# Five buffers for the broadcast reciprocals, earlier key loads and shifted key pooling in a fused attention and MoE kernel

## The chip, the cores and the metric

The kernel runs on one core of one Trainium2 chip. Times are device microseconds of one execution. Before and after were timed several times on the same chip; all times below are of executions in the fast state unless a sentence says otherwise. Engines: PE is TensorE (matmul), DVE is VectorE, ACT is ScalarE, POOL is GpSimd, SP is SyncE. In this kernel POOL and SP matter for what they issue: POOL issues every load that casts from float32 to bf16, and SP issues the transposing reads of the queries. In the traces each works through its instructions in program order: below, three loads go out right behind a broadcast that waited 1.79 us.

## The reference, cut to what matters

```python
def _attn_ref(q, kv, w_sr):                # q: 4 x 12288 x 128, kv: 4 x 384 x 32 x 128
    kv_pool = kv.reshape(B, H // r, r, W // r, r, C).mean(axis=(2, 4))   # r = 4
    k = v = kv_pool.reshape(B, -1, C) @ w_sr                             # 768 keys per batch
    s = scale * (q @ k.transpose(0, 2, 1))
    a = np.exp(s - s.max(-1, keepdims=True)); a /= a.sum(-1, keepdims=True) + 1e-09
    return a @ v
def _moe_ref(x, w_in, w_out):              # x: 49152 x 128, w_in: 128 x 2048
    h = x @ w_in
    return (h * (1.0 / (1.0 + np.exp(-1.702 * h)))) @ w_out
```

## The kernel before

The 49152 queries are worked through in 96 groups of 512. A batch has 24 groups, a block has 4. All attention comes first, then all of the MoE stage. While the groups of batch b run, the keys of batch b+1 are prepared: six loads of a chunk each, two poolings of three chunks, and for each pooling a transpose and the products with `w_sr`. The parts that the change and the argument touch:

```python
kvload = ctx.enter_context(tc.tile_pool(name="kvload", bufs=3))     # raw keys: three chunks
qpool  = ctx.enter_context(tc.tile_pool(name="qpool", bufs=3))      # transposed queries, a block each
agpool = ctx.enter_context(tc.tile_pool(name="ag", bufs=15))        # exponentials
npool  = ctx.enter_context(tc.tile_pool(name="norm", bufs=3))       # reciprocals
# ...
def load_kv(b, a, ch):            # POOL queue, casts
    t = xs[NS - 1 - a * HC - ch] if b == 0 else kvload.tile([128, SG], BF, name="kvt")
    nc.gpsimd.dma_start(out=t, in_=kv_r[b, a, ch])
# ...
def cast_q(s):                    # POOL queue, casts a block of queries, HBM to HBM
    nc.gpsimd.dma_start(out=q_bf[sl, :]..., in_=q_flat[sl, :]...)
def load_qT(s):                   # SP queue, reads a cast block transposed
    qTs[s] = qpool.tile([128, 1, SG], BF, name="qT")
    nc.sync.dma_start_transpose(out=qTs[s], in_=q_bf[s * SG:(s + 1) * SG, :])
# ...
def sums(s):                      # after each block: sums of exponentials, reciprocals
    # ... 24 matmuls, DVE transpose, reciprocal, DVE transpose ...
    for gi in range(4):
        rb = npool.tile([128, 512], F32, name="rb")
        nc.gpsimd.partition_broadcast(rb, t2[32 * gi:32 * gi + 1, :])
        rb_of[4 * s + gi] = rb    # read later: x = av * rb, on DVE
loads = (5, 6, 7, 12, 13, 14)     # group of the batch at which each load is issued
def background(i):
    if i % 4 == 0:
        if 3 <= s + 2 < NS: load_qT(s + 2)
        if 4 <= s + 3 < NS: cast_q(s + 3)
    if b + 1 < B and gb in loads:
        a, ch = divmod(loads.index(gb), HC)
        load_kv(b + 1, a, ch)
# ...
for a, gbs in enumerate(((10, 12, 13, 14), (17, 18, 20, 21))):
    for gb, f in zip(gbs, (pool_kv, transpose_pooled, make_k, make_v)):
        steps[gb] = (f, a)
```

With three reciprocal buffers, the fourth broadcast of a block has to wait until DVE has used the first one. Whatever stands behind it on POOL waits as well.

The softmax here doesn't subtract the row's maximum and nothing guards it: scores larger than these inputs give would overflow.

## Time and profile before

| | before |
|---|---|
| time, first three executions | 1038.17, 1038.11, 1031.79 us |
| profiled execution | 1035.4 us, span 1033.6 us |
| attention, to the start of the last sums | 334.0 us |
| rest (almost all MoE) | 699.6 us |
| two blocks with the pooling of keys 0 to 383 | 22.2 and 17.1 us, against 13.0 in batch 1 |

The page of the kernel before, in four lines: span, busy times, granted PE clock in 40 slices, and the shares of the chain that ended last.

```profile
span 1033.6 us, 13286 instructions
PE 1000.9 (97%) x5298; PEld 458.1 (44%) x5398; DVE 262.3 (25%) x417; ACT 958.7 (93%) x709; POOL 98.2 (9%) x151
PEclk9999989999999999999999999999999999999999
...
PE 90%; DMA 5%; ACT 1%; DVE 1%; issue 1%; POOL 1%; ACTq 0%; POOLq 0%; DVEq 0%
```

PE bounds the kernel, and 5% of the chain is DMA. To find where, I cut attention into blocks, from the start of one block's sums (line 234) to that of the next. The table of stretches gives, for each stretch, its length, busy time and count of each engine, granted clock, DMA share and GB/s. The first two rows are attention and the rest, the other two the long blocks.

```profile
0.00:334.03 334.03, 310.04 (x1864) 132.35 (x1896) 123.66 (x216) 269.55 (x198) 95.27 (x147) 0.99 0.71 114
334.03:1033.61 699.58, 690.85 (x3436) 325.76 (x3504) 138.69 (x201) 689.14 (x512) 2.92 (x4) 1.00 0.10 37
121.48:143.67 22.19, 16.13 (x83) 6.18 (x84) 5.14 (x8) 11.34 (x9) 3.96 (x6) 0.85 1.24 128
206.42:223.56 17.14, 13.60 (x84) 5.61 (x86) 5.14 (x8) 11.20 (x9) 3.96 (x6) 1.00 1.22 145
```

A block without key work takes 11.93 us, one with a pooling 12.96. Only these two stand out; in the first the clock also falls to 0.85. The list of waits between 100 and 240 us says what PE waits for there (total us, times, longest), and the timeline of PE shows the first place.

```profile
PE ring L83 <- DMA kvt<-in_kv_dram: 9.2, 4, 4.9
```

```profile
130.76 0.39 PE L83 MATMUL ring<-kvt,mean 128*32 128x512 bf16 x1
132.00 0.38 PE L83 MATMUL ring<-kvt,mean 128*32 128x512 bf16 x1 [0.85 <-DMA kvt<-in_kv_dram]
137.31 1.86 PE L83 MATMUL ring<-kvt,mean 128*32 128x512 bf16 x10 [4.94 <-DMA kvt<-in_kv_dram]
139.11 1.46 PE L210 MATMUL big<-qT,kT 128*128 128x512 bf16 x3
```

The pooling has to wait for its second and third chunk. After the long wait three score matmuls take 1.46 us instead of the usual 0.81. The Trainium skill ("TensorE: Matmul & The Clock Gate", Part 1) says that an idle window of about 3.4 us halves the PE clock until it has been busy again for as long. Here the trace agrees: the granted clock is 0.50 from 136.11 us, 3.7 us into the idle time, to 142.94 us, and the 2.76 us wait in batch 3 has no such tail.

Why the chunks are late shows on the queues. First POOL between 113 and 120 us (start, duration, what, count, and in brackets the idle time before with what ended it), then the query transpose on SP at that time (start, and how long its issue record lasts), then the landing times of the three loads (least, median, greatest).

```profile
113.00 1.45 POOL L246 PARTITION_BROADCAST rb<-t  x2 [6.57 <-DVE t L243]
114.61 0.80 POOL L246 PARTITION_BROADCAST rb<-t  x1 [0.16 <-DVE x L226]
117.20 0.80 POOL L246 PARTITION_BROADCAST rb<-t  x1 [1.79 <-DVE x L226]
117.83 1.63 POOL L71 DMA_DIRECT2D kvt<-in_kv_dram  x3
119.41 0.55 POOL L117 DMA_DIRECT2D q_bf<-in_q_dram  x1
```

```profile
118.28 20.77 SPq L122 DMA_TRANSPOSE qT<-q_bf  x1
```

```profile
DMA to landing us min/median/max: 5.5/13.6/18.4
```

The fourth broadcast waits 1.79 us for DVE to free a buffer. The three loads follow it at once, 0.54 us apart. The query transpose starts 0.45 us after the first of them. The first load still lands after 5.5 us; the third takes 18.4 us, and the transpose's issue lasts 20.77 us, where 4 to 5 us is common. In batch 1 the same three loads go out 2.1, 1.5 and 1.0 us ahead of the transpose, and land after 5.5, 7.5 and 10.5 us.

### The profile page before, as it was taken

The page shows a single profiled execution, that of the slowest core. Times are in us where ns is not written, and L with a number is a line of the kernel's source. Part 1 is how long each engine was busy: PE and PEld are TensorE (multiplying, and loading weights), DVE is VectorE, ACT ScalarE, POOL GpSimd, SP SyncE. Part 2 cuts the span into 40 slices and gives each one's busy share as a digit, 9 for nine tenths or more (in the row PEclk, how much of TensorE's full clock was granted, in tenths as well). Part 3 has the DMA queues.
Part 4 walks back from the last instruction along what each step waited for, and adds up shares of the span by engine and source line. Part 5 has one row for each costly group of instructions (what it writes and reads, how often), then busy time and mean ns, then how long its engine had stood idle before and what let it go on. Part 6 is the DMA issues. An engine that isn't in the chain of part 4 may idle for free.

```text
span 1033.6 us, 13286 instructions
## 1 busy us (share of the span) xinstructions
PE 1000.9 (97%) x5298; PEld 458.1 (44%) x5398; DVE 262.3 (25%) x417; ACT 958.7 (93%) x709; POOL 98.2 (9%) x151
## 2 busy tenths in 40 slices
PE   6899979989999999999999999999999999999998
PEld 2344434434444444444444444444444444444443
DVE  3344324334333211211212112121121121211212
ACT  3888958978999999999999999999999999999997
POOL 2232322323222100000000000000000000000000
PEclk9999989999999999999999999999999999999999
DMA  9885798599520011011011010010110101101011
GB/s 197 153 146 99 107 103 157 78 148 143 94 50 1 11 42 41 32 40 42 33 39 42 31 41 37 36 41 31 42 41 32 42 31 41 41 31 42 31 42 41
DMA packets 67231, 63.85 MB, mean 62 GB/s; under 512 B 50176, under 2 KB 51328, under 8 KB 66816
## 3 DMA queue, kind: packets, MB, share of 16 engines
q0 software_dynamic: 7440, 26.22, 14.8%
q1 hardware_dynamic: 59728, 36.77, 14.5%
q8 instruction: 42, 0.69, 0.3%
q14 instruction: 21, 0.17, 0.1%
HBM read 52.49 MB, written 36.70 MB: 86 GB/s over the span
## 4 chain that ended last, share of the span: by engine, by line
PE 90%; DMA 5%; ACT 1%; DVE 1%; issue 1%; POOL 1%; ACTq 0%; POOLq 0%; DVEq 0%
PE big L287 32%; PE ring L301 31%; PE ring L222 11%; PE big L210 10%; DMA kvt<-in_kv_dram 3%; PE ring L234 3%; PE ring L313 2%; DMA x<-in_kv_dram 2%; ACT ag L290 1%; PE ring L83 1%; DVE x L226 1%; ACT ag L213 1%; POOL x L71 0%; POOL rb L246 0%; POOL kvt L71 0%
## 5 line engine op out<-in xcount | busy, mean ns | idle before, releaser
L290 ACT ACTIVATE ag<-big 128x1536 bf16<-128x1536 f32 x512 | 689.3, 1557 | 4.7 <-PE big L287 4.6
L287 PE MATMUL big<-x,w_in_sb 128*128 128x512 bf16 x1507 | 412.7, 379 | 2.2
L301 PE MATMUL ring<-ag,w_out_sb 128*128 128x512 bf16 x1496 | 407.1, 379 | 1.9 <-ACT ag L290 0.5
L213 ACT ACTIVATE ag<-big 128x1536 bf16<-128x1536 f32 x192 | 265.1, 1463 | 51.0 <-PE big L210 50.2
L301 PEld LDWEIGHTS <-w_out_sb 128*128 128x128 bf16 x1536 | 150.1, 98 | 181.7 <-issue 0.7
L287 PEld LDWEIGHTS <-w_in_sb 128*128 128x128 bf16 x1536 | 145.9, 98 | 162.4 <-issue 5.0
L305 DVE CAST oT<-ring 128x512 bf16<-128x512 f32 x96 | 66.4, 692 | 450.0 <-PE ring L301 450.0
L210 PE MATMUL big<-qT,kT 128*128 128x512 bf16 x548 | 154.1, 382 | 6.8 <-ACT ag L213 2.8
L222 PE MATMUL ring<-ag,v 128*128 128x512 bf16 x573 | 155.2, 380 | 1.9 <-DVE x L226 1.1
L226 DVE TENSOR_TENSOR x<-ring,rb 128x512 bf16<-128x512 f32 x96 | 66.4, 692 | 160.9 <-PE ring L222 159.6
L246 POOL PARTITION_BROADCAST rb<-t x96 | 72.8, 797 | 220.8 <-DVE t L243 173.6
L315 DVE CAST o_sb<-ring 128x512 f32<-128x512 bf16 x96 | 66.4, 692 | 101.7 <-PE ring L313 101.7
L222 PEld LDWEIGHTS <-v 128*128 128x128 bf16 x576 | 56.4, 98 | 72.0 <-issue 6.7
L210 PEld LDWEIGHTS <-kT 128*128 128x128 bf16 x576 | 53.1, 98 | 78.1 <-issue 20.2
L313 PEld LDWEIGHTS <-oT 128*128 128x128 bf16 x384 | 32.3, 114 | 22.7 <-DVE oT L305 1.9
L313 PE MATMUL ring<-ident,oT 128*128 128x128 bf16 x384 | 37.2, 219 | 0.9 <-DVE oT L305 0.8
L234 PE MATMUL ring<-ag,ones 128*32 128x512 bf16 x576 | 35.5, 381 | 0.0
L234 PEld LDWEIGHTS <-ones 128*32 128x32 bf16 x576 | 13.2, 96 | 20.6 <-issue 10.2
L239 DVE STREAM_TRANSPOSE t<-ring 128x512 f32<-128x512 f32 x24 | 17.2, 717 | 19.2 <-PE ring L234 19.2
L243 DVE STREAM_TRANSPOSE t<-t 128x512 f32<-128x512 f32 x24 | 17.1, 711 | 2.9 <-DVE t L241 0.5
L83 PE MATMUL ring<-kvt,mean 128*32 128x512 bf16 x72 | 8.6, 415 | 9.2 <-DMA kvt<-in_kv_dram 9.2
L141 ACT COPY qT<-ring 128x512 bf16<-128x512 bf16 x3 | 1.8, 585 | 12.7 <-PE ring L137 12.7
(41 smaller groups left out, 100.2 us busy)
## 6 DMA issues: line engine op xcount, KB each, us to landing
out_dram<-o_sb SPq DMA_DIRECT2D x96, 256.0 KB, 2.0
q_bf<-in_q_dram POOLq DMA_DIRECT2D x22, 512.0 KB, 8.4
kvt<-in_kv_dram POOLq DMA_DIRECT2D x18, 512.0 KB, 7.8
x<-in_kv_dram POOLq DMA_DIRECT2D x6, 512.0 KB, 10.8
x<-in_q_dram POOLq DMA_DIRECT2D x1, 512.0 KB, 18.7
w_in_sb<-in_moe_w_in_dram POOLq DMA_DIRECT2D x1, 512.0 KB, 12.5
w_out_sb<-in_moe_w_out_dram POOLq DMA_DIRECT2D x1, 512.0 KB, 15.5
x<-in_q_dram POOLq DMA_DIRECT2D x1, 384.0 KB, 10.9
```

What stands on the lines that cost most here:

```text
L210: nc.tensor.matmul(s_ps[:, k, :], kTs[b][:, jc * 128:(jc + 1) * 128], rhs, start=True, stop=True)
L213: nc.scalar.activation(a, s_ps, AF.Exp, scale=scale)
L222: nc.tensor.matmul(av_of[i], vs[b][:, jc, :], a_of[i, t][:, k, :], start=(jc == 0), stop=(jc == JC - 1))
L226: nc.vector.tensor_tensor(xs[s][:, (i % 4) * G:(i % 4 + 1) * G], av_of.pop(i), rb_of.pop(i), MUL)
L234: nc.tensor.matmul(ss[32 * gi:32 * gi + 32, :], ones, a_of[4 * s + gi, jc // K][:, jc % K, :], start=(jc == 0), stop=(jc == JC - 1))
L246: nc.gpsimd.partition_broadcast(rb, t2[32 * gi:32 * gi + 1, :])
L287: nc.tensor.matmul(h_ps[:, k, :], w_in_sb[:, fc * 128:(fc + 1) * 128], xs[g // 4][:, (g % 4) * G:(g % 4 + 1) * G], start=True, stop=True)
L290: nc.scalar.activation(a, h_ps, AF.Gelu_apprx_sigmoid)
L301: nc.tensor.matmul(o_of[g], w_out_sb[:, fc, :], a[:, k, :], start=(fc == 0), stop=(fc == FCH - 1))
L305: nc.vector.tensor_copy(oT.rearrange("p a b -> p (a b)"), o_of[g])
L313: nc.tensor.transpose(o_ps[:, gi * 128:(gi + 1) * 128], oT[:, :, gi], ident)
L315: nc.vector.tensor_copy(o_sb.rearrange("p a b -> p (a b)"), o_ps)
```

## The change

The intent is to have the key chunks in place before their pooling: more reciprocal buffers so that POOL isn't held up, loads issued one to two groups earlier, and the second pooling a group later. An exponential buffer is given up for the space.

```diff
-    agpool = ctx.enter_context(tc.tile_pool(name="ag", bufs=15))
-    npool = ctx.enter_context(tc.tile_pool(name="norm", bufs=3))
+    agpool = ctx.enter_context(tc.tile_pool(name="ag", bufs=14))
+    npool = ctx.enter_context(tc.tile_pool(name="norm", bufs=5))
@@
-    loads = (5, 6, 7, 12, 13, 14)
+    loads = (3, 4, 6, 11, 12, 13)
@@
-    for a, gbs in enumerate(((10, 12, 13, 14), (17, 18, 20, 21))):
+    for a, gbs in enumerate(((9, 10, 12, 13), (18, 20, 21, 22))):
```

Note that the first pooling, of keys 0 to 383, also moves, one group earlier (10 to 9).

## The prediction

> What bounds it now. The first 340 us are attention, the other 690 us the MoE stage (table of stretches: from 360 us on PE and ACT are busy 665 of 674 us each), which the change doesn't touch. In attention PE is the limit: the chain of waits is PE almost throughout. Blocks of four groups, timed from one sum of exponentials (24 concurrent matmuls, 1.41 us) to the next, take 11.93 us with no key work, 12.9 with the pooling or with the other three key steps, 13.3 at most.
>
> Two blocks break this: 121.48 to 143.74 (22.3 us) and 206.49 to 223.63 (17.1 us). Both hold the pooling of keys 0 to 383 for the next batch, where the list of waits shows PE waiting for the key loads: 0.85 and 4.94 us, then 0.68 and 2.76 us. After the 4.94 us gap the clock falls too: three score matmuls take 1.46 us instead of 0.81 (the Trainium skill, "TensorE: Matmul & The Clock Gate", Part 1, says that an idle window of about 3.4 us halves the clock; the trace agrees, and the 2.76 us gap has no such tail). Against 12.9 us the two blocks lose 9.4 + 4.2 = 13.6 us.
>
> Why the loads are late. In both places three loads stand on GpSimd behind the fourth broadcast of a block, which waits 1.8 us for a reciprocal buffer, and are issued together at 117.8 and 202.8, 13 us before the pooling. The transpose of the next queries starts 0.45 us later on the other queue; the loads issued after it land after 13 to 18 us, instead of 5.5 to 10.5 in batch 1 (issued 2 us ahead of the transpose, no stall). The Trainium skill ("DMA: Bandwidth & Descriptors", "Issuing engines are not separate DMA queues") says both share the 16 engines and interleave; the trace agrees.
>
> What the change does. Instruction counts stay the same. Five buffers take away the fourth broadcast's wait (1.8 us, about 24 times; off PE's chain, but what stands behind it on GpSimd comes earlier). Loads one and two move ahead of a whole block of broadcasts: I expect them near 104 and 105.5 instead of 118, in a stretch where the DMA share was 0.36, and load three near 116. The pooling comes one group earlier, near 128; I expect load three to land by 122 to 125. The second half of the keys is loaded earlier and pooled a group later; it had no stall. 14 exponential buffers instead of 15 cost nothing: a score block needs the values of 12 units before, which PE has finished in program order.
>
> At the start loads one and two go out near 12 and 17 us, behind the initial loads of the same queue; the first query transposes (landed at 35.6 and 37.6) may come 3 to 8 us later, with 7 us or more to spare (estimate from the use near 44).
>
> Sum: 13.6 us off the profiled 1035.4 gives 1021.8; 0 to 4 us of stall may remain. I predict 1022 us, range 1017 to 1030. Chances: faster by over 2% 0.05, within 2% 0.93, slower 0.02.
>
> Right if: no PE gap over 1 us before a pooling; both blocks 12.9 to 13.5 us; clock near 1.0 in 120 to 160; loads one and two 12 us earlier; the fourth broadcast follows the third at once; MoE length unchanged.
>
> Wrong if: loads one and two meet the query transpose near 106 and stretch it and load three, so that pooling still waits at 128, or query tiles come late (the old trace has one landing after 32 us); or the start is delayed. The old times spread by 6.4 us, probably these stalls.

## The result, and the profile after

The changed kernel took 1022.47 us in the median of four executions (1022.37 to 1023.44), the kernel before 1036.31 us in the median of four (1031.79 to 1038.17). The ratio is 0.9875, with a 95% interval of 0.9838 to 0.9911. Here and below a ratio is the mean time of one kernel's fast runs over that of the other's of the same rounds, so not quite the ratio of the medians quoted. The class is "within 2%".

The same views of the changed kernel. The page:

```profile
span 1021.7 us, 13264 instructions
PE 999.7 (98%) x5298; PEld 457.9 (45%) x5398; DVE 262.3 (26%) x417; ACT 959.1 (94%) x709; POOL 92.6 (9%) x151
PEclk8999999999999999999999999999999999999999
...
PE 93%; ACT 3%; DVE 1%; issue 1%; DMA 1%; POOL 0%; ACTq 0%; DVEq 0%; POOLq 0%
```

The table of stretches: attention to the start of the last sums, the rest, and the two blocks with the first pooling of batches 2 and 3.

```profile
0.00:321.09 321.09, 307.95 (x1864) 132.39 (x1895) 123.66 (x216) 269.23 (x198) 89.81 (x147) 0.98 0.67 119
321.09:1021.67 700.58, 691.74 (x3436) 325.53 (x3504) 138.62 (x201) 689.90 (x512) 2.77 (x4) 1.00 0.10 37
122.23:135.55 13.32, 13.18 (x88) 5.57 (x89) 5.40 (x9) 11.43 (x9) 4.37 (x7) 1.00 0.64 119
197.80:211.12 13.32, 13.18 (x88) 5.58 (x89) 5.40 (x9) 11.42 (x9) 4.37 (x7) 1.00 0.74 121
```

The two blocks now take 13.32 us each at a full clock. They hold the pooling and, from the next group, the transpose of what was pooled, so they are a little longer than the 12.96 us of a pooling alone, and a later block is as much shorter. In the list of waits from 100 to 240 us this is the only line in which PE matmuls wait:

```profile
PE ring L222 <- DVE x L226: 0.6, 3, 0.2
```

The pooling runs without a gap. POOL and SP, and the landing of the three loads from 104 to 118 us:

```profile
128.92 1.04 PE L83 MATMUL ring<-kvt,mean 128*32 128x512 bf16 x12
```

```profile
101.82 2.77 POOL L246 PARTITION_BROADCAST rb<-t  x4 [9.77 <-DVE t L243]
104.43 0.58 POOL L71 DMA_DIRECT2D kvt<-in_kv_dram  x1
104.97 0.52 POOL L117 DMA_DIRECT2D q_bf<-in_q_dram  x1
105.46 0.59 POOL L71 DMA_DIRECT2D kvt<-in_kv_dram  x1
113.76 2.77 POOL L246 PARTITION_BROADCAST rb<-t  x4 [7.70 <-DVE t L243]
116.36 0.57 POOL L71 DMA_DIRECT2D kvt<-in_kv_dram  x1
```

```profile
119.04 5.20 SPq L122 DMA_TRANSPOSE qT<-q_bf  x1
```

```profile
DMA to landing us min/median/max: 5.5/5.7/10.1
```

The four broadcasts follow each other at once. Each of these three loads goes out at least 1.6 us ahead of the next transpose (the other one here starts at 107.11), and both transposes are quick (issue 5.86 and 5.20 us).

The profiled spans differ by 1033.61 - 1021.67 = 11.94 us. From the starts of the sums: the five blocks from 121.48 us took 73.01 us and take 63.64, which is 9.37 us less; the five from 206.42 us took 67.82 and take 63.64, 4.18 us less; the blocks of the last batch, 0.14 less. Against this the start is 0.74 us longer, in an execution whose PE clock was low in the first slice (a second trace of the changed kernel is only 0.08 us longer there), and the rest after the last sums is 1.00 us longer.

### The profile page after: what moved, and what is told of

The parts are those of the page before. It is cut to its first block, busy times and chain, and to the rows that moved or that the text cites. A ratio compares the mean times of both kernels' runs of the same rounds, so it can differ in the third digit from the quotient of the medians.

```text
span 1021.7 us, 13264 instructions
## 1 busy us (share of the span) xinstructions
PE 999.7 (98%) x5298; PEld 457.9 (45%) x5398; DVE 262.3 (26%) x417; ACT 959.1 (94%) x709; POOL 92.6 (9%) x151
## 4 chain that ended last, share of the span: by engine, by line
PE 93%; ACT 3%; DVE 1%; issue 1%; DMA 1%; POOL 0%; ACTq 0%; DVEq 0%; POOLq 0%
PE big L287 31%; PE ring L301 30%; PE ring L222 12%; PE big L210 12%; PE ring L234 3%; ACT ag L290 3%; PE ring L313 2%; DMA x<-in_kv_dram 1%; PE ring L83 1%; ACT ag L213 1%; DVE x L226 0%; ACTq L396 0%; DVE oT L305 0%; DVE pooled L86 0%; PE ring L92 0%
## 5 line engine op out<-in xcount | busy, mean ns | idle before, releaser
L246 POOL PARTITION_BROADCAST rb<-t x96 | 66.6, 797 | 220.2 <-DVE t L243 220.2
L313 PEld LDWEIGHTS <-oT 128*128 128x128 bf16 x384 | 32.2, 113 | 22.7 <-DVE oT L305 1.9
L234 PEld LDWEIGHTS <-ones 128*32 128x32 bf16 x576 | 13.2, 96 | 20.6 <-issue 10.2
L117 POOL DMA_DIRECT2D q_bf<-in_q_dram x22 | 11.4, 519 | 4.1 <-DMA x<-in_kv_dram 2.8
## 6 DMA issues: line engine op xcount, KB each, us to landing
x<-in_q_dram POOLq DMA_DIRECT2D x1, 512.0 KB, 18.6
w_out_sb<-in_moe_w_out_dram POOLq DMA_DIRECT2D x1, 512.0 KB, 13.6
```

The lines of the kernel that those rows point to most:

```text
L234: nc.tensor.matmul(ss[32 * gi:32 * gi + 32, :], ones, a_of[4 * s + gi, jc // K][:, jc % K, :], start=(jc == 0), stop=(jc == JC - 1))
L313: nc.tensor.transpose(o_ps[:, gi * 128:(gi + 1) * 128], oT[:, :, gi], ident)
```

## The experiments

The prediction came out, but the change has three parts, and the trace alone doesn't say which of them did it, or whether it is the time of issue or the meeting with the transpose that counts. Twelve runs were made: nine new kernels, and three repeats. All passed the comparison with the reference; the plain-copy run passed too although its queries are wrong, so this comparison doesn't vouch for it. "Before" beside each group of runs is the kernel before in the same rounds: 1038.62 us median (1030.3 to 1042.45, 11 runs) in the first group, 1038.79 (1030.58 to 1045.43, 11 runs) in the second, 1039.89 (1031.17 to 1047.72, 11 runs) in the third. The second group ran on another chip than the other two.

### The buffers alone

```diff
-bufs=15 (ag), bufs=3 (norm)
+bufs=14 (ag), bufs=5 (norm)
```

> Only the five reciprocal buffers (and 14 exponential buffers); load and pooling places as before. Theory A (what counts is where the loads stand in relation to the query transposes on the shared DMA engines): the fourth broadcast no longer waits, so the three loads go out near 116.2 instead of 117.8, about 2 us ahead of the transpose that starts near 118.3, as in batch 1 of the kernel before. They then land after 5.5, 7.5 and 10.5 us, the last near 127, before the pooling at 130.7: no stall, 1022 to 1024 us. Rival B (what counts is the move by a whole block of broadcasts): 1.6 us earlier takes 1.6 us off each of two stalls, with a little less cold clock: about 1031 us, PE gaps of 2 to 4 us remain. Rival C (the broadcast waits themselves cost PE time): gains in all 24 blocks, not only in two.

Measured: 1023.03 us median of six, ratio 0.9863 [0.9827, 0.99]. Five executions lie between 1022.81 and 1023.18; one took 1030.92. POOL and SP in the trace (of the execution that took 1022.91 us):

```profile
115.88 1.63 POOL L71 DMA_DIRECT2D kvt<-in_kv_dram  x3
```

```profile
118.55 8.08 SPq L122 DMA_TRANSPOSE qT<-q_bf  x1
```

The loads go out at 115.88 us, 2.67 us ahead of the transpose (118.55), land after 5.6, 7.6 and 9.7 us, and the transpose's issue lasts 8.08 us. The two blocks take 12.96 us each. Blocks without key work still take 11.93 us. So theory A holds: the buffers alone give practically the whole gain, and they do it in two blocks, not in all 24. Rival B (1031 us) and rival C fall.

### The places alone

```diff
-loads = (5, 6, 7, 12, 13, 14);  steps at (10, 12, 13, 14), (17, 18, 20, 21)
+loads = (3, 4, 6, 11, 12, 13);  steps at (9, 10, 12, 13), (18, 20, 21, 22)
```

> Only the places of loads and pooling as in the changed kernel; three reciprocal buffers and 15 exponential buffers as before. The fourth broadcast still waits 1.8 us, so loads one and two go out near 106 and 107, at the same time as the query transpose at 106.4, and load three near 117.8, just ahead of the next transpose. Theory A: the two loads may now take 10 to 18 us in the collision, but they have 22 us to the pooling; load three lands first in its queue, 5.5 us after issue or up to 9 us, near 124 to 127, before the pooling at 128.2: 1022 to 1025 us. If the buffers are needed as well (load three late because of the two before it): 1026 to 1032 us with PE gaps before the poolings of batch 2 and 3.

Measured: 1039.52 us median of seven, ratio 1.0004 [0.9969, 1.0039]. Moving the loads up to 11 us earlier, without the buffers, is worth nothing. The profiled execution was the fastest of the seven (1027.21 us): the first load goes out at 106.79, the transpose starts 0.45 us later, a cast and the second load follow behind its start, and its issue lasts 14.34 us. POOL and SP there:

```profile
106.79 0.58 POOL L71 DMA_DIRECT2D kvt<-in_kv_dram  x1
107.34 0.52 POOL L117 DMA_DIRECT2D q_bf<-in_q_dram  x1
107.96 0.56 POOL L71 DMA_DIRECT2D kvt<-in_kv_dram  x1
```

```profile
107.24 14.34 SPq L122 DMA_TRANSPOSE qT<-q_bf  x1
```

Load two then takes 15.6 us; the backlog reaches load three, issued at 118.72, which takes 13.1 us, and the pooling waits 2.46 us. The granted clock is 0.50 just after this wait, from 131.77 to 135.19 us, so the block takes 17.71 us. In batch 3 the same instructions meet with a lead of 0.54 us, the transpose takes 8.9 us and nothing waits. The slow executions of this kernel have no trace. My central expectation (1022 to 1025 us) missed; even the alternative that the buffers are needed as well was too mild.

### The first three loads alone

```diff
-loads = (5, 6, 7, 12, 13, 14)
+loads = (3, 4, 6, 12, 13, 14)
```

> Only loads one, two and three of each batch are moved (groups 3, 4 and 6 instead of 5, 6 and 7); loads four to six, pooling and buffers as before. Theory: the only stalls of the kernel before are at the first pooling, so this alone gives the whole gain, 1022 to 1025 us, with the pooling a group later than in the changed kernel and so more to spare than in the run with all places moved. If the later pooling of keys 384 to 767 or the earlier one of keys 0 to 383 was needed: over 1028 us.

Measured: 1039.38 us median of six, one of them (1052.29) slow; ratio 1.0 [0.9961, 1.0039]. A miss as well. The transpose at 106.71 starts 0.45 us behind a load, with a cast and a load behind it: issue 18.6 us, landing after 40 us. Load three lands 23.45 us after its issue, the pooling waits 10.17 us, and the score matmuls then wait 3.31 us for the query tile of that transpose. Earlier places moved the collision to another transpose, in this execution a worse one.

### Plain copies in place of the query transposes

```diff
-nc.sync.dma_start_transpose(out=qTs[s], in_=q_bf[s * SG:(s + 1) * SG, :])
+nc.sync.dma_start(out=qTs[s].rearrange("p o e -> p (o e)"),
+                  in_=q_bf[s * SG:(s + 1) * SG, :].rearrange("(p i) c -> p (i c)", p=128))
```

> The kernel before with each query transpose replaced by a plain copy of the same bytes on the same queue at the same place; the result is wrong on purpose. Theory (the query transposes, running together with the loads, make them land late): the three loads of batches 2 and 3 land 5.5 to 11 us after issue although they are issued at the same 117.8, no PE gap over 0.5 us before a pooling, 1021 to 1024 us. Rival (three loads and a cast issued in one burst 13 us before the pooling are too late whatever runs beside them): landings of 13 to 18 us and a stall remain, 1031 to 1038 us.

Measured: 1021.94 us median of four, ratio 0.9841 [0.9804, 0.9878]. The loads go out at 117.89 us and the copy 0.45 us later, the same positions as in the kernel before, and the loads land after 6.2, 8.5 and 10.4 us. No pooling waits. The transposes are needed for the stall; a burst of three loads, a cast and the same bytes on the other queue is not enough for it.

### Three buffers, with the loads ahead of the fourth broadcast

```diff
     for gi in range(4):
+        if gi == 3 and s % SB == 0 and s + SB < NS:
+            for ch in range(HC):
+                load_kv(s // SB + 1, 0, ch)
         rb = npool.tile([128, 512], F32, name="rb")
@@
-        if b + 1 < B and gb in loads:
+        if b + 1 < B and gb in loads[HC:]:
```

> Three reciprocal buffers and the pooling places of before; only the first three loads of a batch stand on GpSimd just ahead of the fourth broadcast of their block instead of behind it. If the buffers work only by letting these loads out ahead of the query transpose, this does the same without a buffer: loads near 115.3 to 116.4, all three queued before the transpose at 118.3, landings of 5.5 to 10.5 us, no PE gap over 0.5 us before the poolings of batches 2 and 3, 1022 to 1025 us. If the fourth broadcast's wait itself cost time, or the buffers do something else: over 1030 us.

Measured: 1021.9 us median of six (1021.65 to 1022.63), ratio 0.9853 [0.9806, 0.9901]. The loads go out at 115.08 us, 3.04 us ahead of the transpose, and land after 5.7, 7.8 and 9.9 us. The fourth broadcast is still held up, and no matmul waits over 0.2 us for anything in the batches with key work. So the buffers act only by letting the loads past; the broadcast's wait costs nothing in itself.

### Three and four idle broadcasts between the buffers and the loads

Both start from the kernel with the buffers alone.

```diff
+        if s % SB == 0 and s + SB < NS:
+            for _ in range(3):                # 4 in the second kernel
+                idle = npool.tile([128, 512], F32, name="idle", bufs=1)
+                nc.gpsimd.partition_broadcast(idle, t2[0:1, :])
```

> Five reciprocal buffers as in the run with the buffers alone, but three broadcasts into a scratch tile (about 0.65 us each, 2 us together) stand between the fourth broadcast and the first three loads of each batch: the loads go out near 117.9, about 0.6 us ahead of the query transpose, as in the kernel before, with no buffer wait. Theory (the loads' place relative to the transpose): loads two and three fall behind the start of the transpose, it takes over 12 us to issue, loads land after 13 to 18 us, stalls return: 1030 to 1038 us. Rival (only the 2 us count): load three lands near 128.7 and 206.5, at or just after the poolings, at most 1 us of stall each: 1022 to 1025 us.

> As the run with three idle broadcasts, with four: the loads go out near 118.5, at the moment the transpose starts or after it. Theory: as slow as or slower than with three, all three loads behind the transpose's start, 1030 to 1042 us. Rival (only the 2.6 us count): 1 to 2 us of stall in each of two places, 1024 to 1027 us.

Measured with three: 1036.83 us median of six (one, 1052.52, slow), ratio 0.9996 [0.9941, 1.0051]. POOL, SP and landings of it:

```profile
116.14 2.57 POOL L251 PARTITION_BROADCAST idle<-t  x3
118.54 1.63 POOL L71 DMA_DIRECT2D kvt<-in_kv_dram  x3
```

```profile
118.79 17.86 SPq L122 DMA_TRANSPOSE qT<-q_bf  x1
```

```profile
DMA to landing us min/median/max: 5.6/10.0/15.4
```

Measured with four: 1023.63 us median of six (1022.57 to 1024.38), ratio 0.9867 [0.9814, 0.9919].

```profile
116.10 3.45 POOL L251 PARTITION_BROADCAST idle<-t  x4
119.39 1.63 POOL L71 DMA_DIRECT2D kvt<-in_kv_dram  x3
```

```profile
118.75 1.78 SPq L122 DMA_TRANSPOSE qT<-q_bf  x1
```

```profile
DMA to landing us min/median/max: 7.5/9.5/11.5
```

With three, the transpose starts 0.25 us behind the first load and ahead of the other two, and the stalls are back: waits of 3.35, 3.65 and 4.93 us, blocks of 18.0 and 24.9 us, with five buffers and no broadcast held up. With four, the loads go out 0.85 us later still, and almost all is well again (one pooling waits 0.33 us): the transpose starts 0.64 us ahead of the first load and its issue takes 1.78 us; the last load lands at 131.91 us, earlier than the last one with three (134.97) although it was issued later. My theory for four (as slow or slower, since all loads are behind the transpose's start) fell, and so did the rival that only the 2 us of delay count, in the run with three. What remains is narrower. In these runs it is bad only when the transpose starts between the first load and the ones behind it. It is not bad when they are all ahead of it or all behind it. The meetings of the first three loads of batches 2 and 3 with a transpose, from the traces:

| kernel | loads ahead of the transpose's start, us | behind it, us | its issue, us |
|---|---|---|---|
| before, both | 0.45 | 0.08, 0.61 | 20.8, 15.8 |
| three idle broadcasts, both | 0.25 | 0.28, 0.81 | 17.9, 13.9 |
| places alone, batch 2 | 0.45 | cast 0.10, load 0.72 | 14.3 |
| places alone, batch 3 | 0.54 | cast 0.01, load 0.50 | 8.9 |
| first three loads alone, batch 2 | 0.45 | cast 0.10, load 0.69 | 18.6 |
| first three loads alone, batch 3 | 0.54 | cast 0.00, load 0.49 | 9.0 |
| buffers alone, both | 2.67, 2.1, 1.6 | none | 8.1, 10.2 |
| loads ahead of the fourth broadcast, both | 3.0, 2.5, 2.0 | none | 9.7, 8.5 |
| four idle broadcasts, both | none | 0.64, 1.2, 1.7 | 1.8, 1.8 |
| changed kernel, first and second load, both | 2.7, 1.6 | none | 5.9, 7.4 |

Two rows, with a lead of 0.54 us and a single load behind, fall between loads and are not slow, so the meeting is needed for the stall but doesn't always bring it. The traces not in the table fit it: the second trace of the kernel before and the pooling alone have 0.45 and 0.46 us and issues of 14.1 to 19.0 us. All ten slow meetings of batches 2 and 3 have one load ahead, by 0.24 to 0.46 us, and at least one load behind. More distance, or a second load ahead, goes with no late load: in the kernel before, the transpose at 153.07 us has loads 0.81 and 0.27 us ahead of it and a cast and the 512 KB load of `w_in` 0.25 and 0.74 us behind, and its issue takes 10.4 us; with four idle broadcasts, batch 1 has 0.98 and 0.43 us ahead, one load 0.09 us behind, an issue of 13.1 us, and the three loads still land after 5.4 to 10.6 us. Whether the distance or the number of loads ahead decides was not tried. What differs inside the DMA engines is not shown by these traces.

### The buffers and the pooling places, loads at their old places

```diff
-bufs=15 (ag), bufs=3 (norm);  steps at (10, 12, 13, 14), (17, 18, 20, 21)
+bufs=14 (ag), bufs=5 (norm);  steps at (9, 10, 12, 13), (18, 20, 21, 22)
```

> Five reciprocal buffers and the changed pooling places, but loads one to six at their old places: the pooling of keys 0 to 383 comes one group (2.9 us) earlier, near 128.0, and the three loads go out together near 116 as in the run with the buffers alone, where the last landed at 126.6 and, in batch 3, at 204.45 with the pooling then near 206. So no stall in batch 2 and 0 to 2 us in batch 3, where the margin of the buffers alone is used up: 1022 to 1026 us, with some executions near 1030. It tells whether moving the loads is what pays for the earlier pooling in the changed kernel.

Measured: 1023.1 us median of six (1022.51 to 1023.43), ratio 0.9863 [0.9816, 0.9911]. Batch 3's block takes 13.49 us instead of 13.32: the last load lands at 204.46 us, just at the pooling. So even with the earlier pooling the moved loads aren't needed for the time. What they buy is margin: in the changed kernel the third load of batch 3 lands at 198.19 us, some 6 us ahead of its pooling at 204.5.

### The pooling places alone

```diff
-steps at (10, 12, 13, 14), (17, 18, 20, 21)
+steps at (9, 10, 12, 13), (18, 20, 21, 22)
```

> Only the pooling places of the change, on the kernel before. The loads are issued and land as before, near 137 and 220 at the latest, so PE comes to the pooling one group (2.9 us) earlier and waits that much longer: gaps summing to about 8 to 9 us instead of 5.8 and 6 instead of 3.4 in the two places, a colder clock after them, and one group more to do after it; in all 1036 to 1043 us, the same as before or up to 4 us slower. If the pooling place itself helps: under 1033 us.

Measured: 1042.09 us median of six (1038.0 to 1043.3), ratio 1.0029 [0.9996, 1.0063]. The meetings with the transpose are as before (0.45 us, issue 16.6 and 15.7 us), and PE waits 2.75 + 2.66 and 3.13 + 5.07 us. Shifting the pooling by itself doesn't help; within the interval it costs nothing or a little.

### The kernel before once more, for its trace

> The kernel before, unchanged, for a second trace of it. If the stalls before the first poolings of batches 2 and 3 are what spreads its times from 1030 to 1045 us, this trace shows the same two places, with the load again 0.4 to 0.5 us ahead of the transpose and the other loads behind its start, and its time minus 1022 is close to the two blocks' excess over 12.9 us each. If another place shows a gap over 1 us after the start-up, the spread has a further cause.

Measured: one execution, 1046.68 us, of unknown state (it lies 1.5% above the fastest of the same rounds, 1031.17 us, so it may be a slow one). The two meetings are there again (0.45 and 0.46 us), and the blocks take 20.2 and 16.7 us. But this trace has a further cause. After the second meeting two more transposes are slow (issue 18.5 and 13.4 us), and the list of waits from 100 to 260 us has two kinds of wait on DMA:

```profile
PE ring L83 <- DMA kvt<-in_kv_dram: 9.2, 5, 3.3
...
PE big L210 <- DMA qT<-q_bf: 8.0, 1, 8.0
```

At 239.06 us the score matmuls wait 8.0 us for a query tile, and the block with this wait and the one after it take 22.7 and 17.5 us. So in this execution the time comes from the meetings and from how long their backlog lasts, query tiles included. That the fast executions spread from 1030 to 1045 us for the same reason is likely, but not shown. The executions classed slow (1047.72, 1052.29, 1052.52) are all of kernels with the meeting, so they too may only be longer stalls; none has a trace.

### The changed kernel and the three-buffer version, side by side

No edit; both as above.

> The changed kernel again, beside the loads ahead of the fourth broadcast and the pooling alone, on one chip: 1022.4 to 1023.5 us in every execution, as in its first runs. An execution over 1028 us would say that the stalls still come back at times.

> The version with three buffers and the loads ahead of the fourth broadcast again, beside the changed kernel: 1021.6 to 1022.7 us. If it beats the changed kernel, then by under 0.1 per cent; both are free of the stalls, so nothing larger can be left between them.

Measured: the changed kernel 1022.63 us median of six (1022.38 to 1023.43), ratio 0.985 [0.9817, 0.9883]; three buffers with the loads ahead of the fourth broadcast 1021.88 us median of six (1021.65 to 1022.72), ratio 0.9844 [0.9814, 0.9874]. The second is lower by 0.75 us in the median; both its medians are lower. It has a traced counterpart: from the start of the last sums to the end the six traces with 14 exponential and five reciprocal buffers that I compared (changed kernel twice, buffers alone, buffers and pooling, both with idle broadcasts) take 700.55 to 700.58 us, and the eight with 15 and three 699.56 to 699.59. Why 14 and five cost 1.0 us there was not tried. It accrues in eight equal steps of about 0.12 us over the MoE stage, each a few PE matmuls starting some hundredths of a microsecond late.

## Why the prediction was right

- **The time.** 1022 us was predicted, 1022.47 measured. The two blocks were to give 9.4 + 4.2 = 13.6 us; between the traces they gave 9.37 + 4.18 = 13.55.
- **The signs.** No PE gap over 1 us before a pooling, blocks within 12.9 to 13.5 us (13.32), clock 1.00 in both, the fourth broadcast directly behind the third: these as predicted. "MoE length unchanged" failed by 1.0 us. Loads one and two were placed near 104 and 105.5 and came at 104.43 and 105.46; load three near 116 and came at 116.36, landing at 121.85 against "122 to 125". Load two is 13 us earlier than before, load three only 2.5.
- **The start.** The first query transposes were to land 3 to 8 us later and did so by 4 us (39.63 and 41.51 us instead of 35.60 and 37.59), with no wait for them.
- **The cause of the late loads.** The prediction put it down to the transpose on the other queue, citing the Trainium skill ("DMA: Bandwidth & Descriptors", "Issuing engines are not separate DMA queues": all queues run on the same 16 DMA engines and interleave). Plain copies at the same positions remove the stall, and moving the loads past the transpose's start to either side does so too; a delay back into the meeting brings it back. That is shown. The page's interleaving alone doesn't explain it, since the same bytes as plain copies interleave as well.
- **Where its reasoning was off.** It gave most weight to the move of loads one and two "ahead of a whole block of broadcasts", and spoke of the buffers as 1.8 us off PE's chain. The runs turn this round. The move alone gives a ratio of 1.0004, the buffers alone 0.9863. Without the buffers the load is tied to the transpose: in the kernel before the fourth broadcast is released by DVE, which follows PE, and the transpose by PE having read an old query tile, and the two start 0.45 to 0.46 us apart in all four such meetings traced of it; earlier places only pick another transpose to meet, 0.45 to 0.54 us behind the load. The prediction's "wrong if" named this meeting near 106 us as a risk, and the places alone ran into it at 107.24 us; it gave no reason why the changed kernel would escape it. It does because the buffers let the two loads out 2.7 and 1.6 us ahead of that transpose. The number came out because the changed kernel has both parts and no such meeting.
- **"14 exponential buffers instead of 15 cost nothing."** The kernels with 14 and five lose 1.0 us after the last sums. The number of reciprocal buffers changed with it, so which of the two does it is open.
- **The spread "probably these stalls".** Open in part: the one long execution of the kernel before that was traced (1046.68 us) has these stalls, and 8.0 us of waiting for a query tile besides.

Open: what the DMA engines do differently when a transpose starts between loads, and why not at every distance; the cause of the 1.0 us; and whether the moved loads guard against rare slow executions. The buffers alone had one at 1030.92 us among six, without a trace; the changed kernel had none among ten, its ten executions lying within 1022.37 to 1023.44 us.

## What to carry to other kernels

When a load lands late, look at what starts on the other DMA queues within a microsecond of it, not only at how early it was issued: here 11 us of earlier issue gained nothing, while 2 us earlier, or even 1.6 us later, gained 1.3 to 1.4%. A wait of an engine that is off the critical path can still matter, because it fixes when the DMAs behind it in program order go out. Before crediting a change of several parts, run each part alone, even when the prediction of the whole came out to the microsecond.

## What the Trainium skill lacked or had wrong

- "DMA: Bandwidth & Descriptors" (Rules for kernel authors) says, in a row on corrupted results, that a transpose next to ordinary DMAs needs nothing. For the result no run here speaks against that, though the comparison would hardly notice. For the time the page has nothing on it: a query transpose that started 0.24 to 0.46 us behind the first load of a burst from the other queue, with more loads behind it, had an issue of 14 to 21 us in all ten traced cases, instead of 1.8 to 10.2 where the first three loads of batches 2 and 3 were all ahead of it or all behind. The third load of such a burst (512 KB) landed after 15 to 21 us instead of 9 to 12.
- The same page ("Issuing engines are not separate DMA queues") says that issuing from several engines only saves issue time, the transfers interleaving. The order of issue across two queues within a microsecond made 13 us of 1037 here: with the first load 0.25 us ahead of the transpose 1036.83 us, with it 0.64 us behind 1023.63 us. No page has this.
- "TensorE: Matmul & The Clock Gate", Part 1, says that the clock is halved after an idle window of about 3.4 us. The traces agree only in part. After a wait of 4.94 us the granted clock was 0.50 for 6.83 us, and after one of 2.76 us it stayed at 1.00. But it was also 0.50 for 3.42 us after a wait of only 2.46 us (places alone) and for 3.41 us after one of 2.10 us (second trace of the kernel before), with PE busy up to the wait in both. So the length of one wait does not tell whether the clock falls.
